# Linear attention with mixture of experts: in slots of 192 rows, the next chunk's subtraction behind the present sums, and the third expert's rows turned at the front of a step

## Chip, cores, metric

One NeuronCore of a Trainium2 chip runs the whole kernel. The metric is the time of one execution on the device in microseconds (us); a kernel's time is the median of several executions. PE is TensorE, DVE is VectorE, ACT is ScalarE, POOL is GpSimd, SP is SyncE with its DMA queue.

## The reference

```python
proj = einsum('bhsd,df->bhsf', x, w_phi)            # phi of q and of k
proj -= max(abs(proj), -1);  phi = concat(exp(proj), exp(-proj))
kv = phi(k)^T v;  z = sum_s phi(k)
attn = (phi(q) kv) / (phi(q) z + 1e-6)              # (8, 8, 576, 64)
x = attn.transpose(0, 2, 1, 3).reshape(4608, 512)
xc = x[x @ w_skip > 0]                              # the other rows are returned as they are
e_idx = argmax(xc @ w_gate);  gate_w = softmax(xc @ w_gate)[e_idx]
y = gate_w * (relu(xc @ w1[e_idx]) @ w2[e_idx])     # 8 experts, 512 -> 1024 -> 512
out = x;  out[x @ w_skip > 0] = xc + y
```

All numbers are float32. The change lies in the expert part alone.

## The kernel before

The first 310 us are the attention, the rows' experts and the tables of who goes where. The rest, from about 320 us, is the expert part, and the change is there.

**Slots.** Rows of one expert are gathered into slots: 256 rows (kinds E and D; the three E slots are filled before all rows are known), 192 rows (kind C) and 128 rows (kind S). The program is one fixed list of 96 *steps*; in each, PE works through one quarter (a *chunk*, 512 KB) of a slot's first or second weight matrix. Steps 0 to 23 are the slots E0, E1, E2 with eight steps each (four with w1, four with w2). Then come C19 (24 to 31), C20 (32 to 39), S27 and C21 between one another (40 to 55; C21's w1 steps are 44, 45, 50, 51), C22 (56 to 63), D0 and S28 (64 to 79), C23 (80 to 87) and D1 (88 to 95). Chunk *n* is the one that step *n* uses.

**Chunks.** `fetch` (lines 187 to 202) loads a chunk by SP's queue into one of a ring of raw buffers. `split` (204 to 219) makes two float32r parts of it: the rounded high part by a copy on ACT (line 212), and the rest by a subtraction (line 217), on DVE in one instruction over 1024 columns, or on POOL in four over 256. The loop at line 1355 splits a chunk up to six steps ahead of its use, and right behind it lets SP load the chunk seven ahead of that one into the raw buffer that the subtraction has then read.

**Steps.** In the loop over the steps (line 1346), the order of the program is the order on each engine (`manual_schedule`, line 1343). A step does, in this order: gathers of later slots; `part`, the splits that are due; PE's matmuls of the step with what follows them on ACT and DVE; and what stands in the list `along` for this step, such as a slot's `rows`.

**A C slot's w1 step** (`mm1`, lines 1064 to 1078): for each of two groups of 128 hidden units, PE writes into one PSUM bank (`hbank`; three banks P in turn and, every fourth time, bank K) four matmuls of 384 columns (line 1071) and four of 192 (line 1074). ACT copies the half that came from the rows' low parts into `hsum` (line 1076), and DVE adds the other half of the bank to it (line 1077), which frees the bank. Then `hidden_c` (lines 976 to 985) makes Relu's high part on ACT (line 981) and its low part in two instructions on DVE (line 983).

**A slot's rows** (`rows`, line 1296; `split_rows`, 237 to 254): PE turns the gathered rows (line 246; eight transposes for 256 rows), ACT copies the high part from PSUM (line 252), DVE subtracts for the low part (line 253), each once for every 128 rows. E2's rows stand in `along` for step 14, so behind that step's matmuls; E2's first w1 step is 16 (lines 1084, 1085 and 1087 of `mm1`). Chunks 17 and 18 are split in step 13 (both on DVE), chunk 19 in step 14 (on POOL), chunk 20 in step 15 (on DVE).

Of the kernel before, what the change touches and what calls it, by code (L numbers as in the profile page):

```python
# [8 lines left out]
F32 = mybir.dt.float32  # L9
# [5 lines left out]
ALU = mybir.AluOpType  # L15
# [3 lines left out]

P = 128  # L20
SLOT = 256
CFG = {'late': 1, 'sp': 1, 'gp': (6, 8, 11, 14, 16, 19, 21), 'rows': 9.0, 'tab': (2, 2, 3, 4, 5, 6, 7, 8, 9, 10, 11, 12, 15, 19, 31), 'ql': 0, 'cp': 0, 'seq': ('E', 'E', 'E', 'C', 'C', 'SC', 'C', 'DS', 'C', 'D'), 'post': (4, 8, 6), 'post2': (3, 5, 5), 'pk': (0, 2, 4), 'man': (3, 38), 'eng': ('PE', 'DVE', 'Activation', 'Pool'), 'nb': {'K': 1, 'O': 1, 'A': 2, 'P': 3, 'U': 2}, 'apools': (('ld', 2), ('hl', 4), ('up', 5), ('zp', 2), ('ep', 7), ('kvp', 5), ('ac', 1), ('xp', 3)), 'mpools': (('wseta', 1), ('mx', 1), ('mo', 2), ('wsetb', 1), ('wsetc', 1), ('rawq', 1)), 'lag': (2, 2, 3, 0), 'order': ('LPv12KQebRcdBuExzwlr', 'LP01aKQ2ebRcdBuExwzyr'), 'vl': 0, 'at': 1, 'eb': (2, 2), 'ub': 4, 'stage': (2, 2, 4, 4), 'stage2': (1, 2, 3, 3), 'dve': ('0', '1', 'ntkq', '2', 'n2', 'tkq', 'n2t'), 'pd': 1, 'vq': 0, 'qq': 1, 'xb': 4, 'whole': 'k', 'vb': 1, 'af': 1, 'wg': 2, 'q0': 1, 'out6': 2, 'ends': {34: '2dcvQeuEFBwlLRPr', 35: 'QcueERwyLXPr', 36: 'cuwRyLPr'}}


@with_exitstack
def kernel(
# [12 lines left out]
    nc = tc.nc  # L39
    B, H, S, D = q.shape  # L40
    NF = w_phi.shape[1]
    E = w_gate.shape[1]
# [39 lines left out]
    ac = pools["ac"]  # L82
# [118 lines left out]
            nc.sync.dma_start(out=raw.rearrange("p (k m) -> p k m", m=DM), in_=src)  # L201
        return which, i, raw

    def split(chunk, eng):
        which, i, raw = chunk
        s = i % 11
        if i == 11:
            rctx.close()
            wpool[1] = ctx.enter_context(tc.tile_pool(name="wset0", bufs=1, side="right", reuse_waits="tile"))
        pair = wpool[1 if s < 2 else 5 if s < 4 else 2 if s < 9 else 3].tile([P, 2, 1024], F32R, tag="w%d" % s, name="w", bufs=1)  # L210
        hi, lo = pair[:, 0], pair[:, 1]
        nc.scalar.activation(out=hi, in_=raw, func=AF.Copy)  # L212

        n = 256 if eng is nc.gpsimd else 1024
        for a in range(0, 1024, n):
            r = slice(a, a + n)
            eng.tensor_tensor(out=lo[:, r], in0=raw[:, r], in1=hi[:, r].bitcast(F32), op=ALU.subtract)  # L217
        w = FC if which == 1 else DM
        return hi.rearrange("p (k f) -> p k f", f=w), lo.rearrange("p (k f) -> p k f", f=w)

# [43 lines left out]
    raws, wts = {}, {}  # L264
# [792 lines left out]
        nc.vector.scalar_tensor_tensor(out=o[r], in0=yl[r], scalar=g, in1=o[r], op0=ALU.mult, op1=ALU.add)  # L1057
        scatter(idx, o[r])

    def mm1(w, xs):  # L1060
        xg, xh, xl, _, x = xs
        n = P + xg[1].shape[0]
        wh, wl = w
        if n < SLOT:

            hsum = mo.tile([P, 2, n], F32, tag="hsum", name="hsum")
            for fi in range(2):
                hp = hbank()
                fs = slice(fi * P, (fi + 1) * P)
                for kt in range(NKT):  # L1070
                    nc.tensor.matmul(
                        hp[:, 0:2 * n], wh[:, kt, fs], x[:, :, kt, 0:n], start=(kt == 0), stop=False)
                for kt in range(NKT):
                    nc.tensor.matmul(
                        hp[:, 0:n], wl[:, kt, fs], xh[:, kt, 0:n], start=False, stop=(kt == NKT - 1))
                nc.scalar.activation(out=hsum[:, fi], in_=hp[:, n:2 * n], func=AF.Copy)
                nc.vector.tensor_tensor(out=hsum[:, fi], in0=hp[:, 0:n], in1=hsum[:, fi], op=ALU.add)
            return hidden_c(hsum)
        hp = hbank()
        for fi in range(2):  # L1080
            o = hp[:, fi * SLOT:(fi + 1) * SLOT]
            fs = slice(fi * P, (fi + 1) * P)
            for kt in range(NKT):
                nc.tensor.matmul(o, wh[:, kt, fs], xh[:, kt, :], start=(kt == 0), stop=False)
                nc.tensor.matmul(o, wh[:, kt, fs], xl[:, kt, :], start=False, stop=False)
            for kt in range(NKT):
                nc.tensor.matmul(o, wl[:, kt, fs], xh[:, kt, :], start=False, stop=(kt == NKT - 1))
        return hidden(hp)
# [195 lines left out]
                regs[x] = weight_regs((eid0 if kind == "E" else eid)[0:1, i:i + 1])  # L1284
            raws[k] = fetch(w, (w1, w2)[w - 1][regs[x]], c)

    def part(k, eng):
        if k < len(steps):
            wts[k] = split(raws.pop(k), eng)

    def gather(x):
        kind, i = x
# [3 lines left out]
    def rows(x):  # L1296
        kind, i = x
        xss[x] = split_rows(xgs[x], pad0[:, i] if kind == "E" else ft[:, i, 2:4])


    FIRST = 4
# [11 lines left out]
        return sum(1 for v in T if v < t)  # L1313


    along, before, gathers = [], [], []

    def at(k, f):
        along.append((k, f))
# [14 lines left out]
    for xs_, back in ((two, 2), (one, 1)):  # L1334
        for n, x in enumerate(xs_):
            if x not in order[0:2]:
                free = end[xs_[n - back]] + LATE if n >= back else 0
                g = free if x[0] == "E" else max(free, made + 1)
                gathers.append((g, x))
                r = max(step_at(T[g] + 8.0), step_at(T[begin[x]] - CFG["rows"]), one_done[order[order.index(x) - 2]] + 1)  # L1340
                at(min(r, begin[x] - 1), lambda x=x: rows(x))
    loose[0] = True
    with tc.manual_schedule():
        nxt = FIRST
        rests[1]()
        for k, (w, x, c) in enumerate(steps):
            kind, i = x
            for f in [f for s, f in before if s == k]:
                f()
            for s, y in gathers:  # L1350
                if s == k and y[0] != "E":
                    gather(y)
            tabled[0] = kind != "E"
            todo = [f for s, f in along if s == k]
            while nxt < len(steps) and nxt <= k + 6 and (nxt <= k + 1 or parted[nxt] <= T[k] + 1.0):
                w_, x_, c_ = steps[nxt]
                v = nxt not in CFG["gp"] if x_[0] == "E" else not (
                    x_[0] == "C" and w_ == 1 and c_ % 2 == 1 or x_[0] == "S" and c_ % 4 == CFG["sp"])
                part(nxt, nc.vector if v else nc.gpsimd)
                for n in range(0) if nxt < 7 else range(12, 15) if nxt == 7 else range(nxt + 7, nxt + 8):  # L1360
                    load(n)
                nxt += 1
            for s, y in gathers:
                if s == k and y[0] == "E":
                    gather(y)
            if w == 1:
                if kind == "S":
                    st = hss.setdefault(x, {})
                    half1(wts[k], xss[x], c, st)
                    if c % 2 == 1:  # L1370
                        st[c // 2] = half1_out(st[c // 2], c // 2)

                        def turn(st=st, g=c // 2):
                            st[g] = half1_turn(st[g])
                        at(k + 1, turn)
                else:
                    with tc.issue_after(q_last[0].ins) if k == 0 and CFG["af"] else ExitStack():
                        hss.setdefault(x, []).append(mm1(wts[k], xss[x]) if k >= FIRST else mm1_plain(raws.pop(k), xss[x]))
                    if k < FIRST:
                        load(8 + k)  # L1380
            else:
                if c == 0:
                    ys[x] = [bank("O") for _ in range(1 if kind == "S" else 2)]
                if kind == "S":
                    half2(wts[k], ys[x][0], hss[x], c)
                elif x != last:
                    mm2(wts[k], ys[x], xss[x], hss[x], c)
                elif c == NFC - 1:
                    for sub in range(2):
                        for cc in range(NFC):  # L1390
                            mm2(wts[at_step[2, x, cc]], ys[x], xss[x], hss[x], cc, (sub,))
                        put(ys[x], xss[x], sub)
                if c == NFC - 1 and x != last:
                    def out_rows(x=x):
                        for sub in range(len(ys[x])):
                            if x[0] == "S":
                                store(ys[x][0], xss[x], 0)
                            else:
                                put(ys[x], xss[x], sub)
                    before.append((k + LATE, out_rows))  # L1400
            for f in todo:
                f()
            for s, f in [a for a in along if a[0] == k and a[1] not in todo]:
                f()
# [47 lines left out]
```

## Time and profile before

| | |
|---|---|
| median of 3 runs | 581.87 us (579.68 to 582.03) |
| profiled execution | 578.38 us |
| its span, from the first to the last instruction | 576.2 us |
| granted TensorE clock, mean | 0.987 |
| busy: PE, DVE, ACT, POOL | 522.2, 447.4, 341.9, 282.7 us |
| DMA | 116.25 MB, 202 GB/s over the span |

Instructions are named by engine, line of the kernel and operation, with what is written and what is read. A time in brackets behind an instruction is how long its engine stood idle before it, with what released it. Where an engine works without a break, an instruction's start less the start of the one before is what that one cost; its duration also holds what overlaps with the next.

### The profile page before, as it was taken

The numbers are of one execution on the slowest core, as the hardware profiler recorded it, in microseconds if no ns is written. First come the engines' busy times: TensorE is split into PE (matmuls) and PEld (weight loads), VectorE is DVE, ScalarE is ACT, GpSimd is POOL, SyncE is SP. The second block draws the span as 40 slices with busy tenths as digits, with TensorE's granted clock in tenths as the row PEclk, the third lists the DMA queues.
The fourth block names the chain that finished last, engine by engine and source line by source line (L and its number), as shares of the span: only waits on it lengthen the run. The fifth ranks groups of instructions, "written<-read, shape, count | busy, mean of one in ns | idle before, by whom it ended". The sixth has DMA issues, their size and how long they took to land. (4 is left out here: it accounts for less than half of the span.)

```text
span 576.2 us, 20682 instructions
## 1 busy us (share of the span) xinstructions
PE 522.2 (91%) x8606; PEld 485.4 (84%) x8606; DVE 447.4 (78%) x790; ACT 341.9 (59%) x606; POOL 282.7 (49%) x520
## 2 busy tenths in 40 slices
PE   2888999998999898998989999799999989999993
PEld 2788999888998888998988898699889878988892
DVE  3887788988778887797966897778879898868840
ACT  1457676677666776677665443745676757646620
POOL 4213335635547354564546256683749571558011
PEclk9989999999999999999999999899999999999998
DMA  7878878788987989875367895679577986867400
GB/s 147 176 166 163 168 160 211 194 170 174 243 205 194 195 174 224 201 183 122 130 211 270 251 335 179 180 247 335 167 254 241 325 289 233 276 205 250 171 20 32
DMA packets 151233, 116.25 MB, mean 202 GB/s; under 512 B 91875, under 2 KB 126819, under 8 KB 150114
## 3 DMA queue, kind: packets, MB, share of 16 engines
q1 hardware_dynamic: 140704, 104.51, 66.7%
q0 software_dynamic: 3200, 9.45, 4.6%
q10 hardware_dynamic: 7234, 0.95, 1.0%
q8 instruction: 69, 1.13, 0.8%
q14 instruction: 26, 0.21, 0.1%
HBM read 91.66 MB, written 24.02 MB: 201 GB/s over the span
## 5 line engine op out<-in xcount | busy, mean ns | idle before, releaser
L217 POOL TENSOR_TENSOR w<-wraw_c,w 128x256 fp32r<-128x256 f32 x84 | 81.1, 994 | 54.2 <-ACT w L212 38.4
L405 DVE TENSOR_REDUCE m<-ps_A 128x8 f32<-128x1024 f32 x64 | 77.0, 1203 | 35.7 <-PE ps_A L395 35.7
L217 DVE TENSOR_TENSOR w<-wraw_c,w 128x1024 fp32r<-128x1024 f32 x71 | 94.0, 1340 | 12.8 <-ACT w L212 12.5
L212 ACT ACTIVATE w<-wraw_c 128x1024 fp32r<-128x1024 f32 x92 | 93.8, 1050 | 7.4 <-DMA wraw_c<-in_moe_w_dram 7.4
L476 PE MATMUL ps_K<-vm,ek 128*64 128x65 f32 x2048 | 79.9, 224 | 5.4 <-issue 3.0
L406 DVE TENSOR_TENSOR u<-ps_A,m 128x1024 f32<-128x1024 f32 x64 | 78.3, 1224 | 3.9
L545 PE MATMUL ps_O<-kva,eq 128*64 128x74 f32 x1984 | 76.8, 229 | 4.6 <-issue 4.0
L395 PE MATMUL ps_A<-wsrc,xT 64*128 64x128 f32 x1024 | 73.1, 289 | 7.2 <-DVE u L406 4.5
L476 PEld LDWEIGHTS ps_K<-vm,ek 128*64 128x64 f32 x2048 | 73.0, 140 | 5.5 <-issue 4.7
L545 PEld LDWEIGHTS ps_O<-kva,eq 128*64 128x64 f32 x1984 | 68.8, 136 | 8.2 <-issue 4.6
L395 PEld LDWEIGHTS ps_A<-wsrc,xT 64*128 64x128 f32 x1024 | 65.8, 199 | 10.2 <-DVE u L406 4.8
L437 ACT ACTIVATE eq<-ps_V 128x1024 f32<-128x1024 f32 x64 | 65.7, 1030 | 9.6 <-PE ps_V L428 9.6
L420 ACT ACTIVATE ek<-u 128x1024 f32<-128x1024 f32 x64 | 64.1, 1057 | 2.3 <-DVE u L406 2.3
L1110 PE MATMUL ps_O<-w,hh 128*128 128x512 f32 x160 | 63.7, 398 | 0.0
L1029 POOL DMA_INDIRECT out_dram<-o,si x22 | 28.8, 1307 | 59.5 <-DVE si L1025 46.0
L549 ACT ACTIVATE os<-ps_O 128x296 f32<-128x296 f32 x62 | 26.1, 420 | 48.4 <-PE ps_O L545 46.4
L1115 PE MATMUL ps_O<-w,hlo 128*128 128x512 f32 x120 | 47.2, 394 | 0.0
L1114 PE MATMUL ps_O<-w,hh 128*128 128x512 f32 x120 | 47.0, 391 | 0.0
L524 POOL TENSOR_TENSOR xm<-os,rec 128x512 f32<-128x512 f32 x32 | 33.4, 1045 | 24.9 <-DVE rec L523 21.5
L384 DVE STREAM_TRANSPOSE xT<-raw 128x512 f32<-128x512 f32 x64 | 40.5, 669 | 1.2 <-DMA raw<-in_k_dram 1.2
L476 PE MATMUL ps_K<-vt,ekt 128*64 128x65 f32 x512 | 37.7, 224 | 0.0
L1110 PEld LDWEIGHTS ps_O<-w,hh 128*128 128x128 f32 x160 | 30.1, 188 | 6.1
(283 smaller groups left out, 1084.9 us busy)
## 6 DMA issues: line engine op xcount, KB each, us to landing
wraw_c<-in_moe_w_dram SPq DMA_DIRECT2D x96, 512.0 KB, 5.3
raw<-in_k_dram SPq DMA_DIRECT2D x56, 280.0 KB, 5.3
raw<-in_q_dram SPq DMA_DIRECT2D x120, 72.0 KB, 4.6
xrows<-xm SPq DMA_DIRECT2D x8, 1028.0 KB, 5.8
v<-in_v_dram SPq DMA_DIRECT2D x64, 128.0 KB, 3.4
out_dram<-xm SPq DMA_DIRECT2D x32, 256.0 KB, 4.8
xrows<-xt SPq DMA_DIRECT2D x4, 257.0 KB, 6.0
v<-in_v_dram SPq DMA_DIRECT2D x16, 64.0 KB, 3.1
```

The lines of the kernel that those rows point to most:

```text
L212: nc.scalar.activation(out=hi, in_=raw, func=AF.Copy)
L217: eng.tensor_tensor(out=lo[:, r], in0=raw[:, r], in1=hi[:, r].bitcast(F32), op=ALU.subtract)
L395: nc.tensor.matmul(p[:, hd, j * NF:(j + 1) * NF], xT[r], wsrc[r], start=True, stop=True)
L405: lambda: nc.vector.tensor_reduce(out=m, in_=pv, axis=AX.X, op=ALU.max, apply_absolute_value=True),
L406: lambda: nc.vector.tensor_tensor(out=uu, in0=pv, in1=m.rearrange("p h (j o) -> p h j o", o=1).broadcast_to([P, 2, n, NF]), op=ALU.subtract),
L420: nc.scalar.activation(out=o, in_=uu, func=AF.Exp, scale=(1.0, -1.0)[a])
L437: return [lambda a=a: nc.scalar.activation(out=e[:, a].rearrange("p s g c -> p s (g c)"), in_=t, func=AF.Exp, scale=(1.0, -1.0)[a]) for a ...
L476: nc.tensor.matmul(o[s * 64:s * 64 + 64, hd, half, :], e[:, half, s * 64:s * 64 + 64], x, start=(g == 0), stop=(g == 4))
L545: q_last[0] = nc.tensor.matmul(ov[s * 64:s * 64 + 64, 2 * j + hd, :], e[:, half, s, 4 * hd + 2 * th + j], kva[:, half, 2 * pr + hd, :], st ...
L1110: nc.tensor.matmul(y[sub], hh[:, t], wh[:, fi, :], start=first, stop=False)
L1114: nc.tensor.matmul(y[sub], hh[:, t], wl[:, fi, :], start=False, stop=False)
L1115: nc.tensor.matmul(y[sub], hlo[:, t], wh[:, fi, :], start=False, stop=last)
```

## The change

In the w1 steps of C slots, `split` no longer issues DVE's subtraction at once: it hands it to `mm1` as a function, which calls it behind the two adds of the step and before `hidden_c`. This concerns the 16 subtractions on DVE that are issued in such steps (chunks 30 to 32, 38 to 40, 50, 56, 62 to 65 and 86 to 89); four more there are on POOL (chunks 33, 41, 51, 57) and stay where they are. The loads that follow a split stay where they were in the program; one that refills a raw buffer waits for that buffer's subtraction, wherever it stands. The second part: the `rows` of E2, the only slot of kind E for which the loop orders them, are issued at the front of step 14, ahead of the step's splits and matmuls, instead of at its end.

```diff
+CFG = {'late': 1, 'sp': 1, 'rf': 'E', 'held': 1, 'hk': 0, ...
...
-    def split(chunk, eng):
+    def split(chunk, eng, held=None):
...
+        def rest():
+            for a in range(0, 1024, n):
+                r = slice(a, a + n)
+                eng.tensor_tensor(out=lo[:, r], in0=raw[:, r], in1=hi[:, r].bitcast(F32), op=ALU.subtract)
+
+        if held is None or eng is nc.gpsimd:
+            rest()
+        else:
+            held.append(rest)
...
-    def mm1(w, xs):
+    def mm1(w, xs, held=()):
...
                 nc.vector.tensor_tensor(out=hsum[:, fi], in0=hp[:, 0:n], in1=hsum[:, fi], op=ALU.add)
+
+            for f in held:
+                f()
             return hidden_c(hsum)
...
-                at(min(r, begin[x] - 1), lambda x=x: rows(x))
+                if x[0] in CFG["rf"]:
+                    rowsat.append((min(r, begin[x] - 1), x))
+                else:
+                    at(min(r, begin[x] - 1), lambda x=x: rows(x))
...
             tabled[0] = kind != "E"
+            for s, y in rowsat:
+                if s == k:
+                    rows(y)
+            held = [] if w == 1 and kind == "C" and CFG["held"] else None
...
-                part(nxt, nc.vector if v else nc.gpsimd)
+                part(nxt, nc.vector if v else nc.gpsimd, held if nxt > k + CFG["hk"] else None)
...
+                            mm1(wts[k], xss[x], held or ()) if k >= FIRST else mm1_plain(raws.pop(k), xss[x]))
```

## Rows read from the trace of the kernel before

**Rows 1.** Waits of PE, 320 to 577 us: engine, line, releaser: total us, times, longest
```profile
PE ps_P L1071 <- DVE hsum L1077: 3.6, 4, 1.5
PE ps_P L1084 <- ACT x L252: 2.9, 1, 2.9
```
**Rows 2.** Timeline of PE in C20: start us, us, instruction, count [idle before]
```profile
418.84 0.58 PE L1074 MATMUL ps_P<-x,w 128*128 128x192 f32 x4
419.26 0.89 PE L1071 MATMUL ps_P<-x,w 128*128 128x384 f32 x4
420.00 0.58 PE L1074 MATMUL ps_P<-x,w 128*128 128x192 f32 x4
421.30 0.97 PE L1071 MATMUL ps_P<-x,w 128*128 128x384 f32 x4 [0.72 <-DVE hsum L1077]
```
**Rows 3.** Timeline of DVE in C20, steps 32 and 33
```profile
416.48 1.21 DVE L217 TENSOR_TENSOR w<-wraw_c,w 128x1024 fp32r<-128x1024 f32 x1
417.61 0.60 DVE L1077 TENSOR_TENSOR hsum<-ps_P,hsum 128x192 f32<-128x192 f32 x2
418.81 0.46 DVE L983 SCALAR_TENSOR_TENSOR hlo<-hsum,hh 128x256 fp32r<-128x256 f32 x1 [0.59 <-ACT hh L981]
...
420.90 0.35 DVE L1077 TENSOR_TENSOR hsum<-ps_P,hsum 128x192 f32<-128x192 f32 x1
```
**Rows 4.** Timeline of ACT in C20, steps 32 and 33
```profile
418.25 0.53 ACT L981 ACTIVATE hh<-hsum 128x384 fp32r<-128x384 f32 x1 [1.92 <-DVE hsum L1077]
...
419.63 0.31 ACT L1076 ACTIVATE hsum<-ps_P 128x192 f32<-128x192 f32 x1
```
**Rows 5.** Timeline of PE in C22 (three rows) and C23 (the last)
```profile
472.19 0.97 PE L1071 MATMUL ps_P<-x,w 128*128 128x384 f32 x4 [1.51 <-DVE hsum L1077]
...
475.49 0.97 PE L1071 MATMUL ps_P<-x,w 128*128 128x384 f32 x4 [0.75 <-DVE hsum L1077]
...
483.27 0.48 PE L1110 MATMUL ps_O<-w,hh 128*128 128x512 f32 x1
...
531.77 0.97 PE L1071 MATMUL ps_P<-x,w 128*128 128x384 f32 x4 [0.60 <-DVE hsum L1077]
```
**Rows 6.** Timeline of DVE in C21 and at the start of C22
```profile
442.35 2.52 DVE L217 TENSOR_TENSOR w<-wraw_c,w 128x1024 fp32r<-128x1024 f32 x1 [0.21 <-ACT w L212]
...
460.53 2.02 DVE L983 SCALAR_TENSOR_TENSOR hlo<-hsum,hh 128x256 fp32r<-128x256 f32 x1 [0.59 <-ACT hh L981]
...
470.66 1.21 DVE L217 TENSOR_TENSOR w<-wraw_c,w 128x1024 fp32r<-128x1024 f32 x1
```
**Rows 7.** Timeline of PE: E2's rows turned, and the start of step 16
```profile
359.05 1.03 PE L246 MATMUL ps_U<-ident,xg 128*128 128x128 f32 x8
...
367.89 0.38 PE L1084 MATMUL ps_P<-x,w 128*128 128x256 f32 x1 [2.87 <-ACT x L252]
369.08 0.39 PE L1085 MATMUL ps_P<-x,w 128*128 128x256 f32 x1 [0.81 <-DVE x L253]
```
**Rows 8.** Timeline of ACT around E2's rows
```profile
363.95 2.93 ACT L212 ACTIVATE w<-wraw_c 128x1024 fp32r<-128x1024 f32 x3
366.79 1.05 ACT L252 ACTIVATE x<-ps_U 128x512 fp32r<-128x512 f32 x2
```
**Rows 9.** Timeline of DVE around E2's rows
```profile
365.02 2.81 DVE L217 TENSOR_TENSOR w<-wraw_c,w 128x1024 fp32r<-128x1024 f32 x2 [2.47 <-ACT w L212]
367.75 1.27 DVE L253 TENSOR_TENSOR x<-ps_U,x 128x512 fp32r<-128x512 f32 x2
```
**Rows 10.** Stretches: busy us (instructions) of PE, PEld, DVE, ACT, POOL; granted clock; DMA; GB/s
```profile
369.90:373.30 3.40, 3.40 (x19) 3.40 (x18) 3.40 (x10) 0.79 (x1) 2.92 (x5) 0.54 0.84 242
373.30:376.70 3.40, 3.40 (x29) 3.40 (x29) 1.94 (x3) 1.74 (x3) 2.87 (x4) 0.96 1.01 279
```
**Rows 11.** Gathers of E2's rows on POOL (line 230), 348 to 352 us
```profile
L230 POOL DMA_INDIRECT xg<-xrows,idg x2: 1013/1150/1288, 349.2 to 350.5; - x2
...
DMA to landing us min/median/max: 6.0/6.3/6.6
```

More of the change, by code (lines that the diff above doesn't have):

```diff
@@ L21 @@
 SLOT = 256
-CFG = {'late': 1, 'sp': 1, 'gp': (6, 8, 11, 14, 16, 19, 21), 'rows': 9.0, 'tab': (2, 2, 3, 4, 5, 6, 7, 8, 9, 10, 11, 12, 15, 19, 31), 'ql': 0, 'cp': 0, 'seq': ('E', 'E', 'E', 'C', 'C', 'SC', 'C', 'DS', 'C', 'D'), 'post': (4, 8, 6), 'post2': (3, 5, 5), 'pk': (0, 2, 4), 'man': (3, 38), 'eng': ('PE', 'DVE', 'Activation', 'Pool'), 'nb': {'K': 1, 'O': 1, 'A': 2, 'P': 3, 'U': 2}, 'apools': (('ld', 2), ('hl', 4), ('up', 5), ('zp', 2), ('ep', 7), ('kvp', 5), ('ac', 1), ('xp', 3)), 'mpools': (('wseta', 1), ('mx', 1), ('mo', 2), ('wsetb', 1), ('wsetc', 1), ('rawq', 1)), 'lag': (2, 2, 3, 0), 'order': ('LPv12KQebRcdBuExzwlr', 'LP01aKQ2ebRcdBuExwzyr'), 'vl': 0, 'at': 1, 'eb': (2, 2), 'ub': 4, 'stage': (2, 2, 4, 4), 'stage2': (1, 2, 3, 3), 'dve': ('0', '1', 'ntkq', '2', 'n2', 'tkq', 'n2t'), 'pd': 1, 'vq': 0, 'qq': 1, 'xb': 4, 'whole': 'k', 'vb': 1, 'af': 1, 'wg': 2, 'q0': 1, 'out6': 2, 'ends': {34: '2dcvQeuEFBwlLRPr', 35: 'QcueERwyLXPr', 36: 'cuwRyLPr'}}
+CFG = {'late': 1, 'sp': 1, 'rf': 'E', 'held': 1, 'hk': 0, 'gp': (6, 8, 11, 14, 16, 19, 21), 'rows': 9.0, 'tab': (2, 2, 3, 4, 5, 6, 7, 8, 9, 10, 11, 12, 15, 19, 31), 'ql': 0, 'cp': 0, 'seq': ('E', 'E', 'E', 'C', 'C', 'SC', 'C', 'DS', 'C', 'D'), 'post': (4, 8, 6), 'post2': (3, 5, 5), 'pk': (0, 2, 4), 'man': (3, 38), 'eng': ('PE', 'DVE', 'Activation', 'Pool'), 'nb': {'K': 1, 'O': 1, 'A': 2, 'P': 3, 'U': 2}, 'apools': (('ld', 2), ('hl', 4), ('up', 5), ('zp', 2), ('ep', 7), ('kvp', 5), ('ac', 1), ('xp', 3)), 'mpools': (('wseta', 1), ('mx', 1), ('mo', 2), ('wsetb', 1), ('wsetc', 1), ('rawq', 1)), 'lag': (2, 2, 3, 0), 'order': ('LPv12KQebRcdBuExzwlr', 'LP01aKQ2ebRcdBuExwzyr'), 'vl': 0, 'at': 1, 'eb': (2, 2), 'ub': 4, 'stage': (2, 2, 4, 4), 'stage2': (1, 2, 3, 3), 'dve': ('0', '1', 'ntkq', '2', 'n2', 'tkq', 'n2t'), 'pd': 1, 'vq': 0, 'qq': 1, 'xb': 4, 'whole': 'k', 'vb': 1, 'af': 1, 'wg': 2, 'q0': 1, 'out6': 2, 'ends': {34: '2dcvQeuEFBwlLRPr', 35: 'QcueERwyLXPr', 36: 'cuwRyLPr'}}
 @with_exitstack
@@ L214, in split @@
         n = 256 if eng is nc.gpsimd else 1024
-        for a in range(0, 1024, n):
-            r = slice(a, a + n)
-            eng.tensor_tensor(out=lo[:, r], in0=raw[:, r], in1=hi[:, r].bitcast(F32), op=ALU.subtract)
+        def rest():
[6 more added lines that the diff above has]
+            held.append(rest)
         w = FC if which == 1 else DM
@@ L1285, in load, with part @@
             raws[k] = fetch(w, (w1, w2)[w - 1][regs[x]], c)
-    def part(k, eng):
+    def part(k, eng, held=None):
         if k < len(steps):
-            wts[k] = split(raws.pop(k), eng)
+            wts[k] = split(raws.pop(k), eng, held)
     def gather(x):
@@ L1313, in step_at @@
         return sum(1 for v in T if v < t)
-    along, before, gathers = [], [], []
+    along, before, gathers, rowsat = [], [], [], []
     def at(k, f):
@@ L1377 @@
                     with tc.issue_after(q_last[0].ins) if k == 0 and CFG["af"] else ExitStack():
-                        hss.setdefault(x, []).append(mm1(wts[k], xss[x]) if k >= FIRST else mm1_plain(raws.pop(k), xss[x]))
+                        hss.setdefault(x, []).append(
+                            mm1(wts[k], xss[x], held or ()) if k >= FIRST else mm1_plain(raws.pop(k), xss[x]))
                     if k < FIRST:
```

## The prediction

> **What bounds the kernel now.** I read the waits of PE first, then the timeline around each of them, then the timelines of the engine that released each. From 320 us on, where the expert part runs, PE works nearly without a break, so the end moves with PE: each microsecond that PE stands still is paid in full, since the last store only follows the last matmul. The waits of PE in that stretch are few [rows 1]: four on the sum `hsum` of a C slot (3.6 us together, longest 1.5), one on the copy of the third expert's turned rows (2.9) and one on the low half of those rows (0.81 [rows 7]). The change has one edit for each of the two causes. So the question is how much of 3.6 and of 3.7 us each edit really takes away.
>
> What a stop costs: in C20 a group of four L1074 matmuls takes 0.42 us from its start to the next group's (418.84 to 419.26). At 420.00 the same group is followed by 421.30, so 1.30 - 0.42 = 0.88 us are lost, 0.16 more than the idle time of 0.72 that is noted on the row [rows 2]. With 0.16 on each, the four stops cost 0.88 + 1.67 + 0.91 + 0.76 = 4.22 us (the other three in [rows 5]).
>
> **Edit 1, the subtraction behind the sums.** It adds no instruction and removes none: 16 subtractions L217 of DVE (chunks 30 to 32, 38 to 40, 50, 56, 62 to 65, 86 to 89; the four on POOL stay) go from before the two adds L1077 of their step to behind them. Now a step of a C slot on DVE is: subtraction (1.21), two adds (0.60), a wait of 0.59 for ACT's Relu, the two L983, and so on [rows 3]. The adds of step 32 start at 417.61 and those of step 33 at 420.90, a cycle of 3.29 us. PE needs 2.3 us for such a step: two groups L1071 with 0.74 to the next start and two L1074 with 0.42 [rows 2]. So DVE falls a microsecond behind in each step, and with four banks in turn (three P, one K) PE meets the bank that isn't free yet in the third or fourth step.
>
> Behind the change, for C20: DVE starts the adds at 416.48 instead of 417.61, since both copies of ACT are there, and has done them at 417.1. ACT's copy for the next step comes some 1.73 us behind the adds (adds done at 418.21; copy from 419.63 for 0.31, ended 419.94, [rows 4]), because Relu and the next chunk's rounding stand before it. In that time DVE does the subtraction (1.13 from start to start) and both L983 (some 0.7, an estimate from 0.46 for the wider one [rows 3]), 1.8 us, about the same. The cycle is then 0.6 + 1.85 = 2.5 us instead of 3.29. The first add of step 33 is done at 417.1 + 1.85 + 0.35 = 419.3; PE asks for that bank at 420.42. The stop is gone, with 1.1 us to spare: 0.88 us back.
>
> For C22, DVE comes late to the slot (stores and two subtractions ahead), and is free at 470.66 [rows 6]. The add takes the place of the subtraction: bank free at 471.0, PE starts at 471.05 instead of 472.19. That gives 1.14 of 1.67 us and leaves 0.5. The next bank: adds done at 471.3, plus 1.73 for the copy and 0.35 for the add is 473.4; PE comes at 471.05 + 2.39 = 473.44. So the second stop (0.91) goes whole. In C23 the pattern is that of C20, one stop of 0.76, gone. Sum: 0.88 + 1.14 + 0.91 + 0.76 = 3.7 us; the first group behind a stop is also some 0.08 longer (0.97 against 0.89), so 0.3 more: **4.0 us**. Bounds: 4.5 if C21, where the same edit works on two steps, hands DVE over to C22 earlier by the missing 0.5; 2.0 if only the first bank of each slot gains and the cycle stays where it is.
>
> What is queued behind the held subtraction: on DVE the two L983, whose results PE reads only in the second half of the slot; on POOL nothing. On SP, the fetch that refills the raw buffer of that chunk, seven chunks ahead, waits for this subtraction and every later fetch stands behind it. The subtraction starts later by the 0.6 us of two adds where DVE is behind, and where DVE runs ahead of PE (C19, where PE never waits) by at most one step of PE, 2.3 us. The cover is long: the chunk subtracted at 470.66 is read by PE in the step that begins at 483.27 [rows 5], 11 us later, and its buffer's next load has as many steps again. I cost this at nothing; without that cover it would be 0.6 to 2.3 us for each of five slots.
>
> **Edit 2, the third expert's rows.** Step 14 now begins with the eight transposes, two ACT copies L252 and two DVE subtractions L253, which before stood behind its matmuls. No DMA moves. PE comes to them twelve matmuls of 512 columns earlier than the 359.05 of now [rows 7], by the pitch of L1071 (0.74 us for four of 384) some 2.9 us, at about 356.2. The gathers issued at 349.2 and 350.5 land 6.0 to 6.6 us behind their issue [rows 11], the second at 356.5 to 357.1, so PE may stand for up to 0.9 us there. PE stands still later anyway, for 2.87 us up to 367.89 [rows 7], so this costs nothing at the end.
>
> On ACT the copies move past one instruction, the rounding of chunk 19: three L212 run from 363.95 for 2.93 us, then the two copies at 366.79 [rows 8]. Two of the three (chunks 17 and 18) still stand ahead, so the copies start at about 365.85 and end at 366.9 instead of 367.84. But on DVE nothing changes places: the subtractions of chunks 17 and 18 belong to step 13, run from 365.02 for 2.81 us, and L253 follows at 367.75 without a gap [rows 9]; chunk 19 is POOL's. L253 ends at 369.02 as before. PE's second matmul of step 16 (L1085) reads its result and starts at 369.08 [rows 7]. So the first matmul (L1084) comes 1 us earlier and the second when it did: the wait on ACT becomes a wait on DVE. I take **0 us**, with bounds of 0.3 lost and 0.5 won. POOL's subtraction of chunk 19 and what follows it there start 1 us later; PE reads that chunk three steps behind step 16.
>
> **Sum.** The profiled execution took 578.38 us (span 576.2): 578.38 - 4.0 = 574.4. The median of the runs shown is 581.87, 3.5 above it; carried over, 581.87 - 4.0 = 577.9 us.
>
> **Rivals.** *The rows gain as well.* This needs L253 to come earlier, so DVE to reach it before 367.75, for instance by subtractions that take 1.21 each instead of 1.4. Then up to the 2.87 + 0.81 us of the two waits go [rows 7]. With them goes the slow stretch behind them: from 369.9 the granted clock is 0.54 (the 1.2 GHz level for most of it) and PE gets 19 matmuls through in 3.4 us, where it does 29 in the next 3.4 us [rows 10]; ten matmuls at 0.117 are 1.2 us. Time: 581.87 - 4.0 - 4.9 = 573.0. Against it speaks the closed row of DVE work from 365.02 to 369.02. The Trainium skill (TensorE: Matmul & The Clock Gate, What's actually happening) says that PE's clock falls to half when it has been idle and comes back with work. The trace agrees, with 0.54 right behind the stop; by that rule a stop that only changes its name keeps its slow stretch.
>
> *The edit doesn't shorten the cycle*, because ACT's chain (Relu, rounding, copies) sets it. Then one stop moves to the next bank and at most a microsecond is won: 581.0. For it speaks that ACT's 1.73 us and DVE's 1.8 are nearly equal, so either can be the longer one. Against it, 2.5 is well under 3.29.
>
> *Slower: POOL's work meets the moved instructions.* In the held order a subtraction and an L983 stand between one add and the next. A subtraction of 1.21 us took 2.52 at 442.35, and an L983 of 0.46 took 2.02 at 460.53, both while POOL worked [rows 3, 6]. If both are hit in one step, the cycle is 2.5 + 1.31 + 1.56 = 5.4 us, 2.1 more than now. This decides once a cycle passes 3.29 us. With one such step in each of C20, C22 and C23, less the 1.1 us to spare, PE loses 3 x 1.0 us against now: 584.9. The adds themselves, with one input in PSUM, show no such times. The Trainium skill (SBUF — State Buffer, Who interferes with whom) says that a VectorE instruction with two SBUF inputs and a GpSimd instruction that reads SBUF shut each other out for their whole length. The two long rows agree; by that rule the edit takes the exposed instruction out of the way of this step's bank but leaves it in the way of the next one's. Against this rival: the same collisions are possible in the present order.
>
> **How the numbers follow.** The forecast has 0.60, with a range of its own of 576.5 to 579.5 (gain 2.4 to 4.5, and half a microsecond of spread). The rows gaining too: 0.12. No shorter cycle: 0.20. Slower: 0.08. About 0.5% (2.9 us, bounds 578.96 and 584.78) is what a measurement of this kernel can tell from no change. Faster by more holds 0.54 of the forecast and 0.12: 0.66. Within it lie 0.06 of the forecast, 0.20 and 0.02 of the slower case, 0.28. Slower 0.06. The range goes from 573.5 (half of the second case left out) to 581.5 (nearly all of the third in): 573.5 to 581.5.
>
> **What would show it.** Right: no PE wait on `hsum` but one of about 0.5 us in C22; adds L1077 some 2.5 us apart; ACT's Relu waiting less for the adds. In step 16, L1085 still starts at about 369 behind L253, with the slow clock behind it. Wrong: waits of PE on `hsum` of over 1 us, cycles still above 3 us, or PE waiting for a chunk (`w`); or a step 16 that begins before 368, which would mean that DVE's order there isn't what I read.

## The result and the profile after

The changed kernel took 575.53 us, median of 6 executions (572.73 to 577.62); the kernel before, executed 6 times beside it, 582.22 (579.68 to 583.41). The ratio is 0.9901, 95% interval 0.9876 to 0.9926, so it is faster by 5.8 us (4.3 to 7.2). The profiled execution took 572.73 us, with a span of 570.5 and a granted clock of 0.989.

In the changed kernel the lines move down by 2 to 10: the adds into `hsum` are L1084 (before: L1077), the two groups of matmuls of a C slot's w1 step L1078 and L1081 (L1071 and L1074), the subtraction of a chunk L219 (L217), E2's transposes L253 (L246), ACT's copy and DVE's subtraction of these rows L259 and L260 (L252 and L253), the low part of Relu L990 (L983), the first two matmuls of a step of E2 L1094 and L1095 (L1084 and L1085).

The waits of PE in the expert part of the changed kernel (engine, line, releaser: total us, times, longest), against [rows 1]:

```profile
PE ps_P L1095 <- DVE x L260: 1.8, 1, 1.8
PE ps_P L1094 <- ACT x L259: 1.3, 1, 1.3
PE ps_P L1097 <- POOL w L219: 1.1, 1, 1.1
PE ps_U L253 <- DMA xg<-xrows,idg: 0.4, 1, 0.4
```

The four waits on `hsum` (3.6 us) are gone. The wait for a chunk from POOL (L1097) is not new: PE stood 1.0 us at the same place before (there L1087), which [rows 1] leaves out. The stop at step 16 is still there: its two parts, 2.9 on ACT and 0.81 on DVE before, are now 1.3 and 1.8, with 0.4 on the gathers ahead of them.

The adds of C22 in the changed kernel, from DVE's timeline (start us, us, instruction, count), against [rows 6]:

```profile
466.20 0.34 DVE L1084 TENSOR_TENSOR hsum<-ps_P,hsum 128x192 f32<-128x192 f32 x1
466.47 0.34 DVE L1084 TENSOR_TENSOR hsum<-ps_K,hsum 128x192 f32<-128x192 f32 x1
466.74 1.21 DVE L219 TENSOR_TENSOR w<-wraw_c,w 128x1024 fp32r<-128x1024 f32 x1
467.87 0.42 DVE L990 SCALAR_TENSOR_TENSOR hlo<-hsum,hh 128x256 fp32r<-128x256 f32 x1
468.22 0.28 DVE L990 SCALAR_TENSOR_TENSOR hh<-hsum,hh 128x128 fp32r<-128x128 f32 x1
468.57 0.62 DVE L1084 TENSOR_TENSOR hsum<-ps_P,hsum 128x192 f32<-128x192 f32 x2
```

Two things are to be seen. The add comes first in the step, and the subtraction fills the time in which DVE used to wait 0.59 us for ACT's Relu [rows 3]: there is no bracket on L990. And the next adds stand 2.37 us behind (466.20 to 468.57), where they stood 3.29 apart in C20 of the kernel before.

PE in C22, beside it: the fifth group asks for the bank that the first group used, and starts without a wait.

```profile
467.46 0.58 PE L1081 MATMUL ps_P<-x,w 128*128 128x192 f32 x4
467.88 0.89 PE L1078 MATMUL ps_P<-x,w 128*128 128x384 f32 x4
```

The add of 466.20 had freed that bank at 466.54, 1.3 us ahead. In the kernel before, this group started 1.67 us late [rows 5].

Where the time went, by stretches that I cut at the same PE instructions in each trace (us). The end of attention is taken at the start of its last 32 matmuls, and the last stretch ends with the start of the last matmul:

| kernel | end of attention | from there to the first transpose of C19's rows | from there to the last matmul |
|---|---|---|---|
| before, three traces | 310.74, 310.34, 308.65 | 79.56, 79.62, 79.63 | 176.21, 176.92, 176.24 |
| after, two traces | 309.10, 311.76 | 79.54, 78.29 | 171.97, 171.91 |

The second stretch holds E0 to E2 and thus edit 2; the third holds all C slots and thus edit 1. In the changed kernel the third is 4.2 to 5.0 us shorter. The second is as long as before in one trace and 1.3 us shorter in the other.

### The profile page after: what moved, and what is told of

The parts are those of the page before. It is cut to its first block, busy times and chain, and to the rows that moved or that the text cites. A ratio compares the mean times of both kernels' runs of the same rounds, so it can differ in the third digit from the quotient of the medians.

```text
span 570.5 us, 20673 instructions
## 1 busy us (share of the span) xinstructions
PE 519.5 (91%) x8606; PEld 481.8 (84%) x8606; DVE 447.1 (78%) x790; ACT 342.4 (60%) x606; POOL 274.9 (48%) x520
## 3 DMA queue, kind: packets, MB, share of 16 engines
q8 instruction: 69, 1.13, 0.8%
## 5 line engine op out<-in xcount | busy, mean ns | idle before, releaser
L219 POOL TENSOR_TENSOR w<-wraw_c,w 128x256 fp32r<-128x256 f32 x84 | 76.7, 942 | 55.8 <-ACT w L212 55.7
L219 DVE TENSOR_TENSOR w<-wraw_c,w 128x1024 fp32r<-128x1024 f32 x71 | 93.6, 1335 | 12.0 <-ACT w L212 11.0
L483 PE MATMUL ps_K<-vm,ek 128*64 128x65 f32 x2048 | 81.1, 224 | 8.5 <-issue 5.6
L402 PE MATMUL ps_A<-wsrc,xT 64*128 64x128 f32 x1024 | 70.0, 281 | 6.2 <-DVE u L413 4.1
L402 PEld LDWEIGHTS ps_A<-wsrc,xT 64*128 64x128 f32 x1024 | 63.0, 192 | 10.5 <-DVE u L413 4.9
L1036 POOL DMA_INDIRECT out_dram<-o,si x22 | 26.3, 1195 | 60.8 <-DVE si L1032 46.3
```

The lines of the kernel that those rows point to most:

```text
L402: nc.tensor.matmul(p[:, hd, j * NF:(j + 1) * NF], xT[r], wsrc[r], start=True, stop=True)
L483: nc.tensor.matmul(o[s * 64:s * 64 + 64, hd, half, :], e[:, half, s * 64:s * 64 + 64], x, start=(g == 0), stop=(g == 4))
```

## The experiments

The theory going in: edit 1 gives the gain, because an add that frees a PSUM bank no longer stands behind a subtraction; edit 2 gives nothing, because DVE's order holds L1095 as before. The rivals: edit 2 gives a part of it; edit 1 works by filling the Relu wait and not by the order; POOL takes back some of it.

**One edit alone, and the change again.** `e1_held_only` leaves E2's rows at the end of step 14, `e2_rows_only` leaves the subtraction ahead of the adds, and `e8_after_again` is the changed kernel once more, on another chip than these two.

```diff
 e1_held_only
-CFG = {'late': 1, 'sp': 1, 'rf': 'E', 'held': 1, ...
+CFG = {'late': 1, 'sp': 1, 'rf': '', 'held': 1, ...
 e2_rows_only
-CFG = {'late': 1, 'sp': 1, 'rf': 'E', 'held': 1, ...
+CFG = {'late': 1, 'sp': 1, 'rf': 'E', 'held': 0, ...
```

> The first edit alone (held subtractions; the third expert's rows stand behind step 14's matmuls as in the kernel before). Theory: the whole gain is the first edit's, so this is as fast as the changed kernel, 4.0 to 4.5 us below the kernel before, ratio 0.992 to 0.993; PE has no wait on hsum; the two waits at step 16 are 2.9 and 0.8 us as before. Rival (the rows gave a part of the 5.8 us that the runs show): this is only 2.5 to 3 us below the kernel before, 0.995, or the hsum waits are not all gone.

> The second edit alone (rows at the front of step 14, subtractions not held). Theory: 0 us, within 0.5 of the kernel before (ratio 0.999 to 1.001): step 16's first matmul comes 1 us earlier, its second when it did, since DVE's L253 still stands behind two subtractions. The four hsum waits stay, 3.6 us. Rival: 1.7 us faster, 0.997.

> The changed kernel itself, on the chip and beside the runs that the three others are compared with. All theories: ratio to the kernel before 0.988 to 0.992. What is open is whether the one instruction L990 of C21's first step (0.41 us alone) is again shut out by POOL for 3.7 us, as in two of four traces of kernels with the same order there; then PE stands 1.15 us before L1025.

Measured, each against the kernel before on its own chip: edit 1 alone 576.86 us, ratio 0.9876 [0.9836, 0.9916]; edit 2 alone 582.71, ratio 0.9988 [0.996, 1.0015]; both again 575.65, ratio 0.9875 [0.9847, 0.9903]. Edit 1 alone is worth as much as both. The gain is larger than expected in both runs with edit 1: 0.992 to 0.993 was expected of edit 1 alone, and its interval ends at 0.9916; of this more at the end of the section. The waits of PE with edit 2 alone (columns as above):

```profile
PE ps_P L1078 <- DVE hsum L1084: 3.3, 3, 1.9
PE ps_P L1095 <- DVE x L260: 1.8, 1, 1.8
PE ps_P L1094 <- ACT x L259: 1.2, 1, 1.2
```

The `hsum` waits are back at 3.3 us, and the stop at step 16 is that of the changed kernel. In the trace of edit 1 alone no wait on `hsum` is left, and step 16 has the two waits of [rows 1] and [rows 7], 2.9 and 0.8. So neither edit touches the other's waits. The second one brings the first matmul of step 16 forward but not the second: most of the wait only gets another name.

**What holds step 16.** `e3_rows_first_dve` puts DVE's subtractions of chunks 17 and 18 behind E2's two subtractions L260. `e4_rows_first` splits both chunks a step later, so that ACT's copies of the rows go ahead too.

```diff
 e3_rows_first_dve
+        waiting = []
...
                     rows(y)
+                    for f in waiting:
+                        f()
-            held = [] if w == 1 and kind == "C" and CFG["held"] else None
+            held = waiting if k == 13 else [] if w == 1 and kind == "C" and CFG["held"] else None
 e4_rows_first
-            while nxt < len(steps) and nxt <= k + 6 and (nxt <= k + 1 or ...
+            while nxt < len(steps) and nxt <= k + 6 and not (k == 13 and nxt >= 17) and (nxt <= k + 1 or ...
```

> The changed kernel with DVE's subtractions of chunks 17 and 18 behind the two subtractions of the third expert's rows; ACT's order stays. Theory (DVE's order is what holds step 16): DVE starts the rows' subtraction when ACT's first copy is done, so its end and PE's second matmul come 1.3 us earlier, and the time is 1.3 us (0.2%) below the changed kernel, ratio to the kernel before 0.988; with luck the slow clock behind the stop goes too, another 1.2. Rival (ACT's order, or the gathers, hold step 16): no change against the changed kernel, 0.990.

> The changed kernel with the splits of chunks 17 and 18 (ACT's rounding and DVE's subtraction) one step later, so behind the third expert's rows on both engines. Theory: ACT's copies follow the last of the table's copies directly, 2 us earlier, DVE is free for the rows' subtraction, and PE's stop at step 16 shrinks from 3.1 us of idle time to under 1; the stretch at half clock behind it (1.2 us) goes as well. Time 3.5 to 4.5 us below the changed kernel, ratio to the kernel before 0.982 to 0.984. Rival: chunk 17 now comes late to step 17 and PE waits there for w: gain under 1.5 us, 0.988 or above.

Measured: 573.31 us, ratio 0.9831 [0.9798, 0.9865], and 573.58, ratio 0.9837 [0.9799, 0.9876]. Their intervals overlap with that of `e8_after_again` (from 0.9847), so the run times alone don't set them apart from the changed kernel. The traces do, one of each: from the end of attention to C19's rows they needed 77.55 and 76.49 us, against 79.54 and 78.29 in the two traces of the changed kernel. Of `e4_rows_first` 3.5 to 4.5 us below the changed kernel were expected; 0.9837 against 0.9875 is 2.2 us, and its trace has two waits of PE that the changed kernel's has not, 1.0 us for chunk 21 on POOL and 1.0 us at L1025, both taken up below. The timelines of the changed kernel around the stop, ACT, DVE and PE:

```profile
364.35 1.05 ACT L259 ACTIVATE x<-ps_U 128x512 fp32r<-128x512 f32 x2
...
363.54 2.82 DVE L219 TENSOR_TENSOR w<-wraw_c,w 128x1024 fp32r<-128x1024 f32 x2 [2.47 <-ACT w L212]
366.28 1.28 DVE L260 TENSOR_TENSOR x<-ps_U,x 128x512 fp32r<-128x512 f32 x2
...
365.46 0.38 PE L1094 MATMUL ps_P<-x,w 128*128 128x256 f32 x1 [1.30 <-ACT x L259]
367.62 0.58 PE L1095 MATMUL ps_P<-x,w 128*128 128x256 f32 x1 [1.77 <-DVE x L260]
```

Those of `e3_rows_first_dve`, DVE and PE (its attention ended 6.6 us later):

```profile
371.80 1.29 DVE L260 TENSOR_TENSOR x<-ps_U,x 128x512 fp32r<-128x512 f32 x2 [3.90 <-ACT x L259]
...
372.31 0.38 PE L1094 MATMUL ps_P<-x,w 128*128 128x256 f32 x1 [1.15 <-ACT x L259]
373.15 0.39 PE L1095 MATMUL ps_P<-x,w 128*128 128x256 f32 x1 [0.46 <-DVE x L260]
```

And those of `e4_rows_first`, DVE and PE:

```profile
365.09 1.29 DVE L260 TENSOR_TENSOR x<-ps_U,x 128x512 fp32r<-128x512 f32 x2 [2.00 <-ACT x L259]
366.52 2.36 DVE L219 TENSOR_TENSOR w<-wraw_c,w 128x1024 fp32r<-128x1024 f32 x2
...
366.14 0.36 PE L1094 MATMUL ps_P<-x,w 128*128 128x256 f32 x1
366.44 0.39 PE L1095 MATMUL ps_P<-x,w 128*128 128x256 f32 x1
```

In the changed kernel ACT has the high part ready at 365.4, but DVE begins the low part only at 366.28, right behind two subtractions that took it 2.74 us. With these behind L260, and nothing else moved, L1095 comes 0.84 us behind L1094 instead of 2.16: the 1.3 us that were expected of `e3_rows_first_dve`. With ACT's copies ahead too, PE starts both without a wait. So DVE's order is what holds L1095, and edit 2 leaves that order alone.

**What in edit 1 does the work.** `e5_behind_hidden` puts the subtraction not only behind the adds but also behind L990, so DVE waits for the Relu as before. `e6_not_c21` keeps the old order in the w1 steps of C21.

```diff
 e5_behind_hidden
+            hs = hidden_c(hsum)
             for f in held:
                 f()
-            return hidden_c(hsum)
+            return hs
 e6_not_c21
-            held = [] if w == 1 and kind == "C" and CFG["held"] else None
+            held = [] if w == 1 and kind == "C" and x[1] != 21 and CFG["held"] else None
```

> The changed kernel with the held subtraction one place further back, behind both L990 of the step, so that DVE stands idle again (0.59 us) while ACT does Relu. Theory (what counts is that the adds do not wait for the subtraction; filling the idle time is the smaller part): the cycle of the adds is 3.0 us, C20 and C23 stay without a stop, C22's second bank comes 0.6 us late; 0.5 to 1.0 us above the changed kernel (ratio 0.990 to 0.993). Rival (the gain comes from filling the wait for Relu): two to three stops come back, 2 to 3 us above the changed kernel, ratio 0.995.

> The changed kernel with the held order in all C slots but C21. Theory (C21 hands DVE over to C22 earlier; that is the 0.5 us by which the forecast was low): one stop of PE on hsum comes back in C22, 0.5 us long, and the time is 0.5 us above the changed kernel. Rival (the rest came from elsewhere): no stop in C22.

Measured: 578.38 us, ratio 0.9913 [0.9889, 0.9937], and 577.31, ratio 0.9921 [0.9894, 0.9949]. First `e5_behind_hidden`, DVE in C22:

```profile
476.10 0.34 DVE L1084 TENSOR_TENSOR hsum<-ps_P,hsum 128x192 f32<-128x192 f32 x1
...
477.30 0.43 DVE L990 SCALAR_TENSOR_TENSOR hlo<-hsum,hh 128x256 fp32r<-128x256 f32 x1 [0.59 <-issue]
...
477.84 1.22 DVE L219 TENSOR_TENSOR w<-wraw_c,w 128x1024 fp32r<-128x1024 f32 x1
478.97 0.62 DVE L1084 TENSOR_TENSOR hsum<-ps_P,hsum 128x192 f32<-128x192 f32 x2
```

The idle 0.59 us is back and the adds stand 2.87 us apart (476.10 to 478.97), yet this trace has no wait of PE on `hsum` either. By its median it is 2.7 us above `e8_after_again`, the 2 to 3 us that the rival named, but not for the rival's reason, since no stop on `hsum` came back. Putting the adds ahead of the subtraction is enough to end the stops; filling the Relu wait adds 0.5 us of reserve to each step. From C19's rows to the last matmul this kernel needed 174.25 us, 2.3 more than the changed one; 1.96 of them are one stop of PE in S27, of which more below:

```profile
PE ps_O L1025 <- DVE hlo L979: 1.8, 1, 1.8
```

In `e6_not_c21` the first stop of C22 comes back, DVE and PE:

```profile
470.27 0.74 DVE L1064 SCALAR_TENSOR_TENSOR o<-yl,xg,o 64x512 f32<-64x512 f32 x1
470.94 0.34 DVE L1084 TENSOR_TENSOR hsum<-ps_P,hsum 128x192 f32<-128x192 f32 x1
...
470.54 0.58 PE L1081 MATMUL ps_P<-x,w 128*128 128x192 f32 x4
471.34 0.96 PE L1078 MATMUL ps_P<-x,w 128*128 128x384 f32 x4 [0.21 <-DVE hsum L1084]
```

L1078 comes 0.80 us behind the group before it, where 0.42 [rows 2] makes no loss: 0.4 us, near the 0.5 expected. (The median is 1.7 us above `e8_after_again`, with overlapping intervals; the trace accounts for 0.7 of it, 172.65 us from C19's rows to the last matmul.) Against the moment at which PE asks for this bank, DVE's first add of C22 is 1.7 us later than in the changed kernel (470.94 with PE asking at 470.96; 466.20 with PE asking at 467.88). So C21's two steps hand DVE over to C22 earlier by 1.7 us, and that closes the first stop of C22.

**POOL beside DVE.** PE's stop at L1025 also stands in `e1_held_only` and `e4_rows_first` (0.97 and 0.98 us idle, 1.1 lost from start to start in both), and in none of the four traces in which all subtractions stood ahead of the adds. The rows of `e1_held_only`, DVE, POOL and PE:

```profile
444.83 1.76 DVE L219 TENSOR_TENSOR w<-wraw_c,w 128x1024 fp32r<-128x1024 f32 x1
446.52 3.74 DVE L990 SCALAR_TENSOR_TENSOR hlo<-hsum,hh 128x256 fp32r<-128x256 f32 x1
450.18 0.28 DVE L990 SCALAR_TENSOR_TENSOR hh<-hsum,hh 128x128 fp32r<-128x128 f32 x1
450.38 0.68 DVE L979 SCALAR_TENSOR_TENSOR hlo<-ps_U,hh 128x512 fp32r<-128x512 f32 x1
...
442.29 7.68 POOL L219 TENSOR_TENSOR w<-wraw_c,w 128x256 fp32r<-128x256 f32 x8
...
451.11 0.50 PE L1025 MATMUL ps_O<-w,hlo 128*128 128x512 f32 x1 [0.97 <-DVE hlo L979]
```

An L990 of 0.42 us took 3.74 and ended 0.3 us behind POOL's eight pieces (450.26 against 449.97); S27's low part L979, which PE needs, stood behind it. To test that POOL is the cause I put its subtraction of chunk 47, which is four of the eight pieces, on DVE. This went into a kernel that joins `e4_rows_first` with chunk 21's subtraction moved from POOL to DVE, since in `e4_rows_first` PE waits 1.0 us for that chunk. Both versions were run:

```diff
 e7_rows_first_21 (beside the line of e4_rows_first)
-CFG = {... 'gp': (6, 8, 11, 14, 16, 19, 21), ...
+CFG = {... 'gp': (6, 8, 11, 14, 16, 19), ...
 e10_47_on_dve (beside both lines of e7_rows_first_21)
-                    x_[0] == "C" and w_ == 1 and c_ % 2 == 1 or x_[0] == "S" and c_ % 4 == CFG["sp"])
+                    x_[0] == "C" and w_ == 1 and c_ % 2 == 1 or x_[0] == "S" and c_ % 4 == CFG["sp"] and nxt != 47)
```

> As e4 (splits of chunks 17 and 18 behind the third expert's rows) and chunk 21's subtraction on DVE in place of POOL, which came 1.2 us late for step 21 in e4. Theory: that wait of PE (L1124 on POOL, 1.0 us) goes and no other takes its place, 1.2 us below e4: ratio to the kernel before 0.981 to 0.983. Rival: DVE's backlog grows by the subtraction and a stop comes back at the head of C19: no gain over e4, 0.984.

> The version with the third expert's rows first (chunk 21 on DVE), and chunk 47's subtraction on DVE in place of POOL, so that POOL no longer works through eight pieces in a row beside C21's first steps. Theory (POOL's pieces shut out L990, which stood 3.7 us in two traces and 3.6 in the one with the subtraction further back): every L990 of C21 takes under 1.2 us and PE never waits at L1025; in time at most 0.5 us, since the collision comes only in some executions. Rival (L990 is held by something else): an L990 or a subtraction of 2 us or more still stands there. DVE's extra 1.2 us could bring a stop of up to 1 us in C21.

Measured: 571.66 us, ratio 0.981 [0.9786, 0.9834], and 569.66, ratio 0.983 [0.9779, 0.9882] (on a chip where the kernel before took 579.37). `e7_rows_first_21` beats the changed kernel, and so the kernel before: it was compared on the same chip as `e8_after_again`, and the two intervals don't touch (up to 0.9834, from 0.9847). For `e10_47_on_dve` there is no such comparison; its interval holds that of `e7_rows_first_21`. All that is left of PE's waits in `e7_rows_first_21`:

```profile
PE ps_P L1097 <- POOL w L219: 1.0, 1, 1.0
PE ps_U L253 <- DMA xg<-xrows,idg: 0.6, 1, 0.6
PE ps_P L1094 <- DVE hlo L979: 0.3, 1, 0.3
```

With chunk 47 on DVE the same place of the order reads, DVE and POOL:

```profile
439.19 1.22 DVE L219 TENSOR_TENSOR w<-wraw_c,w 128x1024 fp32r<-128x1024 f32 x1
440.32 0.42 DVE L990 SCALAR_TENSOR_TENSOR hlo<-hsum,hh 128x256 fp32r<-128x256 f32 x1
...
441.35 3.16 POOL L219 TENSOR_TENSOR w<-wraw_c,w 128x256 fp32r<-128x256 f32 x4 [4.63 <-ACT w L212]
```

POOL has four pieces there instead of eight, and L990 takes its 0.42 us. That alone proves little, since `e7_rows_first_21`, with the eight pieces, had no stop at L1025 either. What tells the traces apart is whether the eight stand back to back. They do in the three with the stop (7.68, 7.68 and, in `e5_behind_hidden`, where the second L990 of a step took 3.60 us, 5.88). In the changed kernel, its repetition, `e3_rows_first_dve` and `e7_rows_first_21` they come as four and four, with a break of 2.0 to 3.7 us for ACT's rounding, as here in the changed kernel:

```profile
438.50 3.91 POOL L219 TENSOR_TENSOR w<-wraw_c,w 128x256 fp32r<-128x256 f32 x4
444.41 3.04 POOL L219 TENSOR_TENSOR w<-wraw_c,w 128x256 fp32r<-128x256 f32 x4 [2.01 <-ACT w L212]
```

There the subtraction beside the first four took 3.52 us instead of 1.2, without holding up PE, and L990 fell into the break.

Eight pieces back to back are not enough for a stop, though. Later in the same trace POOL runs eight without a break, and the two L990 beside them take 0.63 and 0.83 us, POOL and DVE:

```profile
455.93 8.87 POOL L219 TENSOR_TENSOR w<-wraw_c,w 128x256 fp32r<-128x256 f32 x8
...
456.37 0.63 DVE L990 SCALAR_TENSOR_TENSOR hlo<-hsum,hh 128x256 fp32r<-128x256 f32 x1 [0.59 <-ACT hh L988]
456.92 0.83 DVE L990 SCALAR_TENSOR_TENSOR hh<-hsum,hh 128x128 fp32r<-128x128 f32 x1
```

That POOL holds L990 back is read from the times at which both end in three traces; no run forced it. When DVE gets in between POOL's pieces and when not stays open.

**What is not in the traces.** The ratios of the changed kernel, 0.9901 and 0.9875, are 5.8 and 7.3 us; its third stretch gained 4.2 to 5.0. The kernel before was profiled twice more, to see whether its first trace was by chance a short one in that stretch.

> The kernel before, one more execution with its trace. It asks where the 1.5 us are that the runs show beyond the 4.3 us between the two traces. Theory A (the profiled execution of the kernel before was a lucky one): from the first transposes of C19's rows to the last matmul it takes more than the 176.2 us of that trace, 177 to 180, because a stop on hsum can draw a stretch of 3.4 us at half clock behind it, as in the run with the rows alone. Theory B: 176.2 again, within 0.5; then the rest lies elsewhere.

> The kernel before, a further execution with its trace; the same question and the same expectations: theory A 177 to 180 us in at least one of the two, theory B 176.2 within 0.5 in both.

Measured: single executions of 578.81 and 576.45 us. Their third stretch took 176.92 and 176.24 us, against 176.21 in the first trace. That is below theory A's 177 in both, and 0.2 us outside theory B's half microsecond in the first. But there is a fourth trace with the C slots in the old order, that of `e2_rows_only`, and there this stretch took 179.39 us. Behind the stop of C22 (1.85 us) the granted clock fell, and PE stood 0.7 us more in C21. PE in C22, from the end of that stop (columns as in [rows 10]):

```profile
476.06:479.46 3.40, 3.40 (x17) 3.40 (x17) 2.50 (x6) 1.91 (x4) 2.88 (x4) 0.68 1.01 345
```

So the stretch is not steady in the old order, and the three traces of the kernel before may well be short ones. The granted clocks of all executions point the same way. Untraced, the kernel before has a mean of 0.982 to 0.984 on each of three chips, and the changed kernel 0.987 over the six executions of `e8_after_again`; but the three traced executions of the kernel before have 0.986 to 0.989, and each is faster than the median of its own comparison (578.38 against 581.87, 578.81 and 576.45 against 579.37). A slow stretch of 3.4 us at 0.57 lowers the mean of a whole execution by 0.0026 and cost 1.25 us (next section), so 0.004 would be some 2 us; this is an estimate. It would fit executions of the kernel before with more slow stretches than its three traces have, behind a stop on `hsum` as in `e2_rows_only`. It isn't shown, since none of those executions was traced.

The end of attention, whose instructions stand in the same order in all these kernels, lies anywhere from 308.65 to 315.78 us in the 13 traces, and not earlier in the changed kernels than in the others. That spread is larger than what is missing, and the near end of the first interval, 4.3 us, needs nothing more than edit 1. How much of the rest is clock and how much is spread, these runs don't settle.

## Why the prediction was right, point by point

The measured 575.53 us lies in the range of 573.5 to 581.5 and in the case that was put first, 1 us below the range that this case had for itself (576.5 to 579.5; its own terms, 581.87 less 4.5 less 0.5, give 576.9 for the lower end). The traces bear out the mechanism and 4.2 to 5.0 us. What the runs gained beyond that, the sum did not have.

**Edit 1: the mechanism held, one term was too small.** The stops of C20 and C23 and the second of C22 went whole, as the sum had them. The cycle of adds was put at 2.5 us and measured 2.37 in C22: two adds 0.54, subtraction 1.13, two L990 0.70, from start to start and without a gap. That is 0.07 above PE's pace of 2.3, and 1.3 us of reserve cover it for a slot. ACT's Relu waits less for the adds, as forecast: 12.4 us in all instead of 27.2. The term that was mis-sized is the first stop of C22: 1.14 of 1.67 us were counted, and all of it went. The reason was named as the upper bound, an earlier handover from C21 by the missing 0.5 us; it came earlier by 1.7, and without the change in C21 0.4 us of the stop were there again. That makes 4.5 us instead of 4.0, within the 4.2 to 5.0 of the stretch.

**Edit 2: right, at zero.** PE came to the transposes earlier and met the second gather, 0.40 us of the 0.9 at most that were allowed. Counted from the end of attention, L1094 came 0.8 us earlier (56.36 instead of 57.15 us; forecast 1), and L1095 at 58.52 instead of 58.34, with DVE's subtraction of the rows at 57.18 instead of 57.01: unmoved behind its two neighbours, as [rows 9] had it. The experiment that changed DVE's order alone (1.3 us earlier) shows that this was the cause, and not only a wait that happened to come last. Two of the signs named for being wrong came all the same and say little: step 16 begins before 368, at 365.46, because the forecast itself moves its first matmul to 366.9 and the attention ended 1.6 us earlier in this trace; and PE waits for a chunk `w`, as it did before.

**The rivals.** That the rows gain 4.9 us as well fell with `e2_rows_only`, 0.9988 [0.996, 1.0015]; a gain of up to 2.3 us the interval leaves open, but the trace shows none, with 79.79 us from the end of attention to C19's rows against 79.56 to 79.63. That the cycle isn't shortened fell with 2.37 us. The slower case, POOL against the moved instructions, had a real mechanism: it cost 1.1 us at one place in two of the six traces in which all DVE subtractions of C slots stand right behind the adds and chunk 47 is POOL's, and 1.96 in the variant that holds them longer. But it hit S27's low part and never a bank of `hsum`, so at times it costs a quarter of the gain (1.1 of 4.5) and doesn't turn it round. The Trainium skill (SBUF — State Buffer, Who interferes with whom) says that a DVE instruction with two SBUF inputs and a POOL instruction that reads SBUF shut each other out for their whole length. The rows agree, and go further: 3.74 us is more than three of POOL's pieces of 0.96, so DVE didn't get in between two of them there; beside the eight of 455.93 it did.

**What was left out.** The slow stretch behind the step 16 stop was taken as certain. In the two traces of the changed kernel the same stop, 1.3 and 1.77 us in one, 1.42 and 1.76 in the other, was followed once by a slow clock and once not. In all, nine traces have this stop, and behind eight of them the granted clock of the next 3.4 us was 0.50 to 0.66. The stretches of 3.4 us from the start of L1095 on (busy us and instructions of PE, PEld, DVE, ACT, POOL; granted clock; DMA; GB/s), first the changed kernel:

```profile
367.62:371.02 3.40, 3.40 (x17) 3.40 (x18) 3.40 (x10) 1.58 (x2) 3.13 (x4) 0.57 0.86 284
371.02:374.42 3.40, 3.40 (x31) 3.40 (x30) 2.61 (x3) 1.55 (x2) 2.75 (x5) 1.00 0.82 239
```

and then `e8_after_again`:

```profile
370.33:373.73 3.40, 3.40 (x28) 3.40 (x29) 3.40 (x10) 1.95 (x3) 3.14 (x4) 1.00 0.82 276
```

Seventeen matmuls at 0.57, mostly the level of 1.2 GHz, against 28 at 1.00, the level of 2.4 GHz. That is the 1.25 us by which the second stretches of the two traces differ (79.54 and 78.29): eleven matmuls at 0.117 [rows 10] are 1.3 us.

## What to carry to other kernels

On an engine that works in order, put the operation that frees a buffer which the bounding engine is about to ask for ahead of the operation that prepares work for later; the same instructions in another order gave 4.2 to 5.0 us here. Before moving an operation to an earlier place, look at every engine that handles its data: an edit that leaves one of them in its old order only changes the name under which the wait is listed. And count a stop's reach to the next stage: what one slot saves on a shared engine arrives as a head start in the following one (1.7 us from C21 to C22).

## What was not expected of the hardware

- A DVE instruction of 0.42 us took 3.74 us beside POOL's eight pieces back to back. In the changed kernel, where those eight came as four and four, the slowest L990 of this shape took 1.05 us (count: shortest, median, longest in ns, first and last start):

```profile
L990 DVE SCALAR_TENSOR_TENSOR hlo<-hsum,hh x20: 411/418/1047, 396.7 to 531.1; 128x256 fp32r<-128x256 f32 x20
```

- The same order of instructions and the same stop of PE at step 16 were followed by a slow clock in eight traces and not in a ninth. With edit 2 alone a slow stretch came behind C22's stop of 1.85 us as well; behind a stop of 1.87 us at the same place, in the second trace of the kernel before, the clock stayed at 1.00.
- The attention, the same instructions in the same order on every engine, ended between 308.65 and 315.78 us: a spread of 7 us between single executions, as much as this change brings at most. A part of a kernel is compared by its own stretch; two single times would not have shown 4 us.
